# A transformer block on one core: the first product of the second gate/up pass by a second Strassen level, woven into the unit in front, and both F tiles evacuated jointly

## The chip, the cores and the metric

One core of a Trainium2 chip. The metric is device time in microseconds of the whole kernel. Repeats of one kernel scatter by about 1 us.

## The reference

Input 2048 tokens of width D = 1024. A linear-attention block is followed by a gated block, and this case is about the gated block:

```python
x = A_x
h = x + _A_ref(_layernorm(x), A_wqkv, A_wo)
h2 = h + _B_ref(_layernorm(h), B_W_gate, B_W_up, B_W_down)
# _B_ref:  gate = x @ W_gate;  up = x @ W_up      (1024 x 3584 each)
#          gate = gate * (gate > 0)
#          out  = (gate * up) @ W_down            (3584 x 1024)
```

## The kernel before

Strassen's scheme replaces eight block products by seven, at the price of block sums. The kernel uses it for almost all large products. The gate/up product runs in two passes over 1024 tokens each, and each pass has 14 **units**, alternately a gate unit and an up unit. A unit makes seven products P1 to P7 for a pair of F tiles (u = 0, 1), each of eight matmuls of 128x512 (four for each tile), which end in PSUM banks. Copies between banks ("fk1", "fk2") let two results share a partial sum.

In the second pass P5 is itself done by Strassen (the **inner** level: two weight tiles by two halves of K by two halves of the tokens): seven sub-products M1 to M7 of two 128x256 matmuls each, 14 narrow ones instead of eight wide ones. Cut to its order, the unit before is:

```python
sub(cX, B_X, B_(0, 0), A(0, 0), True, "M1")      # sub: 2 matmuls of 256 columns
sub(cD, B_D, G(0), XS(0), False, "M5")
ident_act(c0, cX, ...)                           # ScalarE, "M1c"
p1(0); p1(1)         # prod P1: 4 matmuls of 512 columns; then fk1: bank BA[u] copied to BB[u]
sub(cX, ..., "M6");  s5(1, 0, cX, ...)
sub(c0, ..., "M2")
p2(0)                # P2 on top of P1 in BA[0], evacuated by "h11"
sub(cX, ..., "M7");  s5(1, 1, cX, ...);  s5_add(1)
p6(0); p2(1); p6(1)  # P6 on top of the copy in BB[u]; then fk2: BB[u] copied to BC_[u]
sub(cX, ..., "M4");  sub(cD, ..., "M3")
... # M4c, s5_add(0)
for u in range(2):   # P7 into BB[u], evacuated by "c22" tile by tile (VectorE, + P5's result)
    prod(u, BB[u], t_blk(u, 2), s_blk(2), False, "P7")
    evac5(1, 1, u, bank(BB[u]), B_bank[BB[u]], c22, B_c22, "c22")
... # P3 into BC_[u], evacuated by "c12" in the same way
for u in range(2):   # P4 on top of P7 in BB[u], evacuated by "h21"
    prod(u, BB[u], t_blk(u, 3), a_blk(1, 1), False, "P4")
    evac(0, 1, u, BB[u], "h21")
```

Gate units evacuate with ScalarE's relu. Up units evacuate on VectorE, multiplying by the gate values. VectorE further makes the weight sums of the next unit in between. Every matmul is issued by one helper, so all have one source line (L769 before, L777 after).

Of the kernel before, what the change touches and what calls it, by code (L numbers as in the profile page):

```python
# [132 lines left out]
def bass_sequential_preLN__linear_attn_block__glu_gated_reglu__prompt_kernel(  # L133
# [71 lines left out]
    with es:  # L205
# [90 lines left out]

        RO = sb("RO", [P, NTR * 4 * KH * P], bf16)
# [9 lines left out]
        lx = RW[:, 4 * NW:8 * NW].bitcast(f16).rearrange("p (z j c) -> p z j c", z=2, j=4)  # L307
        sg_g = [RWG[:, x:x + 4 * WDW].bitcast(f16).rearrange("p (j m t) -> p j m t", j=4, t=SHB)
# [12 lines left out]
        RX = sb("RX", [P, (2 * NHR + NOS) * NW], bf16)  # L321
# [118 lines left out]
        B_s5q = [bufs("s5q%d_" % i, 2) for i in range(2)]  # L440
        B_xs5 = bufs("xs5_", 4)
        B_out2 = bufs("out2_", STB)
        B_xr = bufs("xr_", 2)
# [71 lines left out]
        for b_ in B_outst:  # L515
            b_.over = B_E + B_bt + [B_TWq[2]]
        for b_ in B_hnE:
            b_.over = B_o + B_oT
# [152 lines left out]
        def x_wsums(m):  # L671
# [12 lines left out]
            def one():  # L684
                dma(sl_rx[z], r_v[:, 1, :, m, :], xr[:, z].rearrange("p k (h c) -> p (k h) c", c=HNW), "st_rx_%d" % m,
                    reads=[B_xr[z]], writes=B_rscr[1][2 * m:2 * m + 2])
                add(0, q_(0, 1), q_(0, 0))
                add(2, q_(1, 1), q_(0, 1))
# [697 lines left out]
        def x_inner():  # L1386
            def A(t, k):
                return Ssum[:, 0, 2 * k:2 * k + 2, t * SHB:(t + 1) * SHB], [B_S[0]]

            def X(j):  # L1390
                return xs5[:, j], [B_xs5[j]]

            def add(j, x, y, op):
                PL.add("dve", lambda e: e.tensor_tensor(out=xs5[:, j], in0=x[0], in1=y[0], op=op), reads=x[1] + y[1],
                       writes=[B_xs5[j]], name="xs%d" % (j + 1))
            return [lambda: add(0, A(1, 0), A(1, 1), ALU.add), lambda: add(1, X(0), A(0, 0), ALU.subtract),
                    lambda: add(2, A(0, 0), A(1, 0), ALU.subtract), lambda: add(3, A(0, 1), X(1), ALU.subtract)]
# [22 lines left out]
        def ffn_unit(ps_, n, fill, mid):  # L1420
            Lg = (ps_ * NPAIR + n) * 2
# [5 lines left out]
            if ps_ in L2F:  # L1427
                BE, BB = BB, BE
            if up:
                BB, BC_ = BC_, BB  # L1430
            z = n % 2
            fl = (1, 1) if ps_ not in L2F or n == NPAIR - 1 else (1, 0) if up else (2, 1)

# [27 lines left out]
            def prod(u, b, st_, mov, start, name):  # L1461
                (sf, sr), (mf, mr) = st_, mov
                for kk in range(KH):
                    mm(bank(b), sf(kk), mf(kk), start and kk == 0, kk == KH - 1, sr + mr, B_bank[b],
                       "%s%s_%d_%d" % (name, "gu"[up], ps_, n), skip=True)
# [33 lines left out]

            if ps_ in L2F:  # L1500
                cX, cD, c0 = ps[:, BE[1], 0:SHB], ps[:, BE[1], SHB:2 * SHB], ps[:, BE[0], 0:SHB]
                B_X = B_D = B_bank[BE[1]]
                tb = [B_T[kt[0]][0], B_T[kt[1]][0]]

                def sub(dst, bdst, w, x, start, name):
                    for kk in range(2):
                        mm(dst, w[0](kk), x[0](kk), start and kk == 0, kk == 1, w[1] + x[1], bdst,
                           "%s_%d_%d" % (name, ps_, n), skip=True)

                def B_(kh, u):  # L1510
                    return (lambda kk: Tring[:, kt[u], 0, 2 * kh + kk, :]), [tb[u]]

                def G(j):
                    return (lambda kk: g5[:, z, j, kk * P:(kk + 1) * P]), [B_g5[z][j]]

                def A(t, k):
                    return (lambda kk: Ssum[:, 0, 2 * k + kk, t * SHB:(t + 1) * SHB]), [B_S[0]]

                def XS(j):
                    return (lambda kk: xs5[:, j, kk, :]), [B_xs5[j]]  # L1520

                def s5(u, t, src, b, name):
                    ident_act(ftmp[:, u, t * SHB:(t + 1) * SHB], src, [], [b, B_s5q[u][t]], name)

                def s5_add(t):
                    d = ftmp[:, 1, t * SHB:(t + 1) * SHB]
                    PL.add("dve", lambda e: e.tensor_tensor(out=d, in0=cD, in1=d, op=ALU.add), reads=[],
                           writes=[B_D, B_s5q[1][t]], name="s5a%d" % t)
                for u in range(2):
                    for t in range(2):  # L1530
                        B_s5q[u][t].over = [B_s5[u]]

                sub(cX, B_X, B_(0, 0), A(0, 0), True, "M1")
                sub(cD, B_D, G(0), XS(0), False, "M5")
                ident_act(c0, cX, [], [B_X, B_bank[BE[0]]], "M1c")
                p1(0)
                p1(1)
                sub(cX, B_X, G(1), XS(1), False, "M6")
                s5(1, 0, cX, B_X, "M6c")
                sub(c0, B_bank[BE[0]], B_(1, 0), A(0, 1), False, "M2")  # L1540
                fillin(2 if up else 3)
                p2(0)
                go(mid[2])
                sub(cX, B_X, G(2), XS(2), False, "M7")
                s5(1, 1, cX, B_X, "M7c")
                s5_add(1)
                p6(0)
                p2(1)
                p6(1)
                go(mid[0])  # L1550
                sub(cX, B_X, G(3), A(1, 1), False, "M4")
                sub(cD, B_D, B_(1, 1), XS(3), False, "M3")
                e_ = ps[:, BE[0]:BE[0] + 2, 0:SHB]
                PL.add("act", lambda e: e.activation(out=ftmp[:, 0, :].rearrange("p (t c) -> p t c", t=2), in_=e_,
                                                     func=ACTF.Identity), reads=[B_bank[BE[0]]],
                       writes=[B_X, B_s5[0]], name="M4c")
                go(later)
                later.clear()
                fillin(2 if up else 3)
                s5_add(0)  # L1560
                B_s5[1].over = B_s5q[1]
                B_s5[1].w = B_s5q[1][0].w
            else:
                p1(0)
                p1(1)
                fillin(1)
                for u in range(2):
                    prod(u, BE[u], t_blk(u, 0), s_blk(0), True, "P5")
                    ident_act(ftmp[:, u, :], bank(BE[u]), [B_bank[BE[u]]], [B_s5[u]], "s5")
                fillin(1)  # L1570
                p6(0)
                p6(1)
                go(later)
                later.clear()
                fillin(1)
                go(mid[0])
                p2(0)
                go(mid[2])
                p2(1)
                fillin(1)  # L1580
# [6 lines left out]
            fillin(fl[0])  # L1587
# [9 lines left out]
            fillin(fl[1])  # L1597
# [3 lines left out]
            if ps_ > 0 or n < NPAIR - 2:  # L1601
                load_w_next()
                load_w_next()

# [51 lines left out]
        def down_pass(ps_, fill):  # L1656
# [256 lines left out]
            else:  # L1913
                claim(B_W, B_hnT)
                at(0, 3, *l2_sums(q_10, sg_rg2, "sg2", NM - 1, NM))
# [228 lines left out]
        L2F = (1,)  # L2144
# [3 lines left out]
        for p_ in range(NPASS):  # L2148
            fill = []
            for q in range(NPAIR):  # L2150
                if q + 1 < NPAIR:
                    t_ = t_sums((p_ * NPAIR + q + 1) * 2)
                    if p_ in L2F:
                        t_ = t_[0:1] + w_inner(q + 1) + t_[1:]
                    fill = fill + t_
                mid = [[], [], [], [], []]
                if q > 0 and q % 2 == 0:
                    mid[0].append(lambda q=q: hh_sums(q - 2))
                    mid[3].append(lambda q=q: hh_sums(q - 1))
                if p_ == 0:  # L2160
# [15 lines left out]
                    else:  # L2176
# [5 lines left out]
                        else:  # L2182
                            mid[0] = [load_wd_next] * 2 + mid[0] + [w0_, w1_]
                else:
                    if q == 0:
# [3 lines left out]
                    if 1 <= q <= NM:  # L2189
                        w0_, w1_ = x_wsums(q - 1)  # L2190
                        mid[0].append(w0_)
                        mid[1].append(w1_)
                    if q == NPAIR - 1:
                        claim(B_sgg, B_w[2:6])
                        g_ = l2_sums(q_10, sg_rg2, "sg2", 0, NM - 1)
                        mid[0] += g_[0:2]
                        mid[1] += g_[2:4]
                ffn_unit(p_, q, fill, mid)
                if p_ == 1 and q == NM + 1:
                    claim(B_wd[0:NWS - 3], B_xr + flat(B_lx))  # L2200
                    wd_lim[0] = len(WLIST)
                    for _ in range(NWS):
                        load_wd_next()
                if p_ == 1 and q == NPAIR - 1:
                    for i in range(NWX):
# [6 lines left out]
            hh_sums(NPAIR - 2)  # L2212
            hh_sums(NPAIR - 1)
            if p_ in L2F:
                claim(B_V, B_xs5 + flat(B_g5))
            late = []
            if p_ + 1 < NPASS:
# [13 lines left out]
                if p_ + 1 in L2F:  # L2231
                    def claim_xs():
                        claim(B_xs5, B_V)
                        claim(flat(B_g5), B_V)

                    gi = w_inner(0)
                    xi = x_inner()
                    late += [(claim_xs, (6, 0)), (xi[0], (6, 3)), (xi[1], (6, 4)), (xi[2], (6, 4)), (xi[3], (6, 5))]
# [61 lines left out]
```

## Time and profile before

| | before |
|---|---|
| median of the first runs | 722.53 us (722.41 to 722.60) |
| span of the profiled run | 720.5 us |
| PE, VectorE (DVE), ScalarE (ACT) busy | 99%, 82%, 50% |
| second gate/up pass, by PE starts | 474.37 to 640.81 us: 166.44 us |
| one unit of it | 11.89 us |
| granted clock of PE | 1.0 |

How to read it: a PE that is 99% busy says little by itself, since matmul records overlap and their ends are modelled. What says that PE issues without a gap is that the distance between starts equals the number of columns at the full rate.

### The profile page before, as it was taken

How to read it: one execution, taken by the hardware profiler on the slowest of the kernel's cores; microseconds unless marked ns; L12 is line 12 of the kernel's file. 1: busy time of each engine (PE TensorE's matmuls, PEld its weight loads, DVE VectorE, ACT ScalarE, POOL GpSimd, SP SyncE). 2: the span in 40 equal slices, each digit the busy share in tenths (PEclk: the TensorE clock that was granted, in tenths of full speed). 3: DMA queues.
4: the chain of work that ended last, by engine and by line, in shares of the span. 5: the costliest groups of instructions: out<-in, count | busy, mean ns of one | idle time of the engine just before them, and what ended most of it. 6: DMA issues, size and time to landing. Idle time of an engine off the chain costs nothing.

```text
span 720.5 us, 12877 instructions
## 1 busy us (share of the span) xinstructions
PE 714.3 (99%) x4901; PEld 380.0 (53%) x4901; DVE 588.9 (82%) x1030; ACT 358.9 (50%) x626; POOL 110.8 (15%) x178
## 2 busy tenths in 40 slices
PE   8999999999999999999999999999999999999998
PEld 3344444444444444444444568865555555447887
DVE  6988867899776889888988787887889877888885
ACT  4977666764842466677756111035455445423010
POOL 3321100000350103332321001310000000000331
PEclk9999999999999999999999999999999999999999
DMA  9852344015998797999998999994554572037997
GB/s 295 260 113 65 38 136 157 9 30 97 216 202 264 222 284 236 276 320 297 296 281 266 313 251 317 318 215 119 145 169 139 160 245 84 1 95 248 322 323 183
DMA packets 195101, 144.17 MB, mean 200 GB/s; under 512 B 53984, under 2 KB 172512, under 8 KB 195040
## 3 DMA queue, kind: packets, MB, share of 16 engines
q1 hardware_dynamic: 190048, 138.77, 65.9%
q0 software_dynamic: 4032, 3.67, 3.6%
q10 hardware_dynamic: 960, 0.92, 0.4%
q8 instruction: 38, 0.62, 0.4%
q14 instruction: 23, 0.19, 0.1%
HBM read 98.76 MB, written 32.51 MB: 182 GB/s over the span
## 4 chain that ended last, share of the span: by engine, by line
PE 95%; DVE 2%; DMA 1%; ACT 1%; issue 1%; SPq 0%; ACTq 0%
PE ps L769 95%; DMA RAB<-in_A_wqkv_dram 1%; DVE RWG L1016 0%; DVE RE L857 0%; DVE RX L1100 0%; DVE RE L1674 0%; DVE RX L854 0%; DVE RH L1016 0%; ACT RXH L809 0%; DVE RC L991 0%; DVE RW L991 0%; ACT ps L774 0%; PE ps L910 0%; DVE RWG L1614 0%; SPq L567 0%
## 5 line engine op out<-in xcount | busy, mean ns | idle before, releaser
L774 ACT ACTIVATE ps<-ps 128x512 f32<-128x512 f32 (+1 forms) x193 | 108.9, 565 | 220.8 <-PE ps L769 212.1
L769 PE MATMUL ps<-RC,RO 128*128 128x512 f16 x616 | 143.0, 369 | 0.0
L769 PE MATMUL ps<-RH,RWG 128*128 128x512 bf16 x448 | 108.1, 379 | 0.0
L769 PEld LDWEIGHTS ps<-RC,RO 128*128 128x128 f16 x616 | 60.3, 98 | 63.5
L769 PE MATMUL ps<-RC,RWG 128*128 128x512 f16 x320 | 76.9, 379 | 0.3 <-ACT ps L774 0.2
L769 PEld LDWEIGHTS ps<-RH,RWG 128*128 128x128 bf16 x448 | 43.8, 98 | 46.9
L1483 DVE TENSOR_TENSOR RAB<-ps,RAB 128x512 bf16<-128x512 f32 x56 | 37.3, 686 | 31.3 <-PE ps L769 31.3
L769 PE MATMUL ps<-RH,RO 128*128 128x512 bf16 (+1 forms) x256 | 61.2, 379 | 0.0
L1683 POOL DMA_DIRECT2D out_dram<-RX x20 | 17.9, 1281 | 263.7 <-DVE RX L1674 221.5
L769 PE MATMUL ps<-RW,RE 128*128 128x512 bf16 x256 | 57.6, 380 | 0.0
L769 PE MATMUL ps<-RW,RAB 128*128 128x256 f16 (+3 forms) x362 | 52.9, 301 | 0.0
L769 PEld LDWEIGHTS ps<-RC,RWG 128*128 128x128 bf16 (+1 forms) x320 | 30.0, 98 | 40.3 <-ACT ps L774 6.3
L774 ACT ACTIVATE RE<-ps 128x512 f32<-128x512 f32 (+1 forms) x64 | 31.5, 503 | 37.8 <-PE ps L769 37.8
L769 PE MATMUL ps<-RAB 128*128 128x512 bf16 (+2 forms) x238 | 49.8, 348 | 0.0
L769 PEld LDWEIGHTS ps<-RW,RAB 128*128 128x128 f16 (+1 forms) x362 | 35.3, 98 | 14.5
L1674 DVE TENSOR_TENSOR RE<-ps,RE 128x512 f32<-128x512 f32 x44 | 30.2, 686 | 14.2 <-PE ps L769 13.7
L774 ACT ACTIVATE RAB<-ps 128x512 bf16<-128x512 f32 x56 | 33.3, 595 | 16.7 <-PE ps L769 16.4
L1367 DVE TENSOR_TENSOR RO<-RWG 128x1024 f16<-128x1024 bf16 x54 | 36.9, 684 | 4.5 <-DMA RWG<-in_B_W_up_dram 4.5
L769 PEld LDWEIGHTS ps<-RH,RO 128*128 128x128 f16 (+1 forms) x256 | 24.4, 98 | 29.9 <-ACT RX L774 1.5
L1478 ACT ACTIVATE RAB<-RAB 128x1024 bf16<-128x1024 bf16 x28 | 29.5, 1055 | 19.3 <-DVE RAB L1469 18.7
L1469 DVE TENSOR_TENSOR RAB<-ps,RE 128x512 bf16<-128x512 f32 x56 | 37.1, 685 | 2.1 <-PE ps L769 1.7
L769 PEld LDWEIGHTS ps<-RW,RE 128*128 128x128 bf16 x256 | 24.0, 98 | 27.9 <-DVE RXH L1265 0.4
(170 smaller groups left out, 1170.3 us busy)
## 6 DMA issues: line engine op xcount, KB each, us to landing
RWG<-in_B_W_gate_dram SPq DMA_DIRECT2D x28, 512.0 KB, 6.2
RWG<-in_B_W_up_dram SPq DMA_DIRECT2D x28, 512.0 KB, 5.2
RW<-l_scr SPq DMA_DIRECT2D x20, 448.0 KB, 5.6
RW<-in_B_W_down_dram SPq DMA_DIRECT2D x14, 512.0 KB, 5.4
t_scr<-RW SPq DMA_DIRECT2D x14, 512.0 KB, 4.8
l_scr<-RX SPq DMA_DIRECT2D x7, 1024.0 KB, 6.1
RE<-l_scr SPq DMA_DIRECT2D x15, 448.0 KB, 4.9
RE<-in_A_x_dram SPq DMA_DIRECT2D x23, 256.0 KB, 3.7
```

What stands on the lines that cost most here:

```text
L769: lambda e: e.matmul(out_ap, lhsT, rhs, start=start, stop=stop, skip_group_check=skip),
L774: PL.add("act", lambda e: e.activation(out=dst, in_=src, func=func), reads=reads, writes=writes, name=name)
L1367: PL.add(eng, lambda e: e.tensor_tensor(out=tb(j, u), in0=f0(u), in1=f1(u), op=ALU.subtract), reads=[B_w[i + x] for x in r] + ([B_T[k + x] ...
L1469: PL.add("dve", lambda e: e.tensor_tensor(out=d, in0=src, in1=ftmp[:, u, :], op=ALU.add), reads=[bsrc, B_s5[u]], writes=[db], name=name)
L1478: PL.add("act", lambda e: e.activation(out=d, in_=d, func=ACTF.Relu), reads=[], writes=db, name=name)
L1483: PL.add("dve", lambda e: e.tensor_tensor(out=d, in0=bank(b), in1=d, op=ALU.mult), reads=[B_bank[b]], writes=[db], name=name)
L1674: PL.add(eng, lambda e: e.tensor_tensor(out=dst, in0=in0, in1=in1, op=op), reads=reads, writes=writes, name=name)
L1683: PL.add("pool", lambda e: e.dma_start(dst, src, accum_op=ALU.add), reads=[bsrc], writes=[B_hscr[st]], slot=sl, name="acc_%d_%d" % (st, dh))
```

## The change

Its intent: P1 of units 1 to 13 also gets the inner Strassen level (seven sub-products R1 to R7), which takes 512 columns a unit off PE. R1 to R7 are spread over the unit in front, so that the copies between them are covered by other products. To make room on VectorE for the added sums, the two F tiles of a result are evacuated in one instruction, and the PSUM reads of the up units' h11 and h21 go to ScalarE, leaving VectorE a 16-bit multiply.

The core of the diff (buffers, the wide D1/D3 sums of `hh_pair` and the new places of load and sum calls are cut):

```diff
+        def w_inner1(n): ...      # three VectorE sums of the raw weights of unit n: g1
+            go(pre)
             sub(cX, B_X, B_(0, 0), A(0, 0), True, "M1")
-            sub(cD, B_D, G(0), XS(0), False, "M5")
+            sub(cD, B_X, G(0), XS(0), False, "M5")
...
-                p1(0)
-                p1(1)
+            go(late21)                       # h21 of the unit in front
+            if n == 0:                       # only unit 0 still makes its own P1
+                for u in range(2):
+                    prod(u, BA[u], w_blk(u, 0, 0), a_blk(0, 0), True, "P1")
+                    fk1(u, BB)
+            if n > 0:
+                p2()
... # M6, M2, M6c, out11(0), P6(0), fk2(0), M7, M3, s5a
+            if nxt:
+                sub(r0, B_r, Br(0, 0), Ar(0, 0), True, "R1")
+                sub(rX, B_r, Gr(0), XSr(0), False, "R5")
+                ident_act(m5r, rX, [B_r], [B_m5r], "R5c")
+                ident_act(rX, r0, [], [B_r], "R1c")
... # P6(1), fk2(1), M4, out11(1), P7(0)
+                sub(r0, B_r, Br(1, 0), Ar(0, 1), False, "R2")
+                sub(rX, B_r, Gr(1), XSr(1), False, "R6")
+                ident_act(rc, rX, [B_r], [B_y], "R6c")
... # P7(1), c22 of both tiles, P3(0)
+                sub(rX, B_r, Gr(2), XSr(2), False, "R7")
+                sub(rc, B_y, Br(1, 1), XSr(3), False, "R3")
+                dve(... both R banks + m5r ..., "Ra")
... # P3(1), c12 of both tiles, P4(0)
+                sub(rX, B_r, Gr(3), Ar(1, 1), False, "R4")
+                for u in range(2):
+                    fk1(u, BC_)
+            prod(1, BB[1], t_blk(1, 3), a_blk(1, 1), False, "P4")
```

```diff
-                PL.add("dve", lambda e: e.tensor_tensor(out=d, in0=src, in1=ftmp[:, u, :], op=ALU.add), ...
+                dve(d, ps[:, bk[0]:bk[0] + 2, :], ftmp[:, 0:2, :], ...)      # c22, c12: both tiles
```

## The prediction

> **What bounds the kernel now.** I read the page first, then the chain of work that ended last, then the PE timeline of the second gate/up pass, then busy time by stretch. The page (busy time, then the chain by engine) and the chain in order of time:
>
> ```profile
> PE 714.3 (99%) x4901; PEld 380.0 (53%) x4901; DVE 588.9 (82%) x1030; ACT 358.9 (50%) x626; POOL 110.8 (15%) x178
> ...
> PE 95%; DVE 2%; DMA 1%; ACT 1%; issue 1%; SPq 0%; ACTq 0%
> ```
>
> ```profile
> 103.69 0.59 ACT ps L774
> 104.28 0.05 issue
> 104.32 576.26 PE ps L769 x3727
> 680.58 0.02 issue
> 680.60 0.69 DVE RE L1674
> ```
>
> PE works 714.3 of 720.5 us, and one unbroken piece of 576 us of matmuls covers everything this change touches. The second gate/up pass runs from 474.4 to 640.8 us: 14 units of one Strassen step. One whole unit on the PE timeline (start, length, engine, operation, count; the ends are modelled and overlap the next start, so I read starts):
>
> ```profile
> 486.26 0.38 PE L769 MATMUL ps<-RC,RO 128*128 128x256 f16 x2
> 486.48 0.38 PE L769 MATMUL ps<-RE 128*128 128x256 f16 x2
> 486.69 1.89 PE L769 MATMUL ps<-RH,RWG 128*128 128x512 bf16 x8
> 488.42 0.38 PE L769 MATMUL ps<-RE 128*128 128x256 f16 x2
> 488.64 0.38 PE L769 MATMUL ps<-RC,RO 128*128 128x256 f16 x2
> 488.86 1.03 PE L769 MATMUL ps<-RH,RWG 128*128 128x512 bf16 x4
> ...
> 494.69 1.89 PE L769 MATMUL ps<-RC,RWG 128*128 128x512 f16 x8
> 496.42 1.89 PE L769 MATMUL ps<-RH,RO 128*128 128x512 bf16 x8
> 498.15 0.38 PE L769 MATMUL ps<-RC,RO 128*128 128x256 f16 x2
> ```
>
> The line of eight wide matmuls at 486.69 is P1, the product to be changed. Eight 128x512 matmuls take 488.42-486.69 = 1.73 us, 0.2157 each; a pair of 128x256 takes 0.218 us, 0.109 each. A unit is 48 wide and 14 narrow ones: 48 x 0.2157 + 14 x 0.109 = 11.88 us, and the trace has 498.15-486.26 = 11.89. So PE issues with no gap at all, and only fewer columns can shorten this pass. The other engines, unit by unit and then over ten units (stretch, its length, busy us and count of each engine, clock, DMA share, GB/s):
>
> ```profile
> 486.26:498.15 11.89, 11.89 (x64) 6.08 (x63) 7.18 (x15) 5.32 (x10) 0.00 (x0) 1.00 0.30 90
> 498.15:510.04 11.89, 11.89 (x64) 6.07 (x63) 10.90 (x25) 6.61 (x12) 0.00 (x0) 1.00 0.54 154
> 521.93:640.81 118.88, 118.88 (x622) 60.64 (x621) 97.55 (x197) 59.68 (x110) 0.00 (x0) 1.00 0.42 124
> ```
>
> VectorE is the second engine, 97.55/118.88 = 82% busy; ScalarE has half its time free.
>
> **What the Trainium skill says.** "TensorE: Matmul & The Clock Gate", section "Wait — 56ns, not 53.3ns?": start to start is N/2.4 GHz plus about 2.5 ns. That gives 215.8 ns for 512 columns and 109.2 for 256; the trace's 0.2157 and 0.109 agree, and the narrow form pays its fixed 2.5 ns twice. "VectorE: DVE Perf Modes", section "The perf-mode tier table": tensor_tensor on 16-bit SBUF data runs two elements a cycle, with a PSUM operand one. The trace agrees: 1024 elements SBUF to SBUF 684 ns, 512 from PSUM 685 ns, 1024 from PSUM 1219 ns; so two 512 evacuations joined save 2 x 685 - 1219 = 0.15 us. "PSUM — Partial Sum Buffer", section "PSUM bank collisions raise a hardware error": PSUM is to be guarded by bank. The kernel does so (one tracker a bank), hence the new copies in one bank become waits of PE if they come late; nothing in the profile before shows the new ones.
>
> **The change part by part.**
> PE. In units 0 to 12 the P1 of the following unit (8 wide matmuls) becomes seven sub-products R1 to R7 of two narrow ones each; unit 0's own P1 stays direct. The built programs, counted by shape, agree: wide 2571 to 2467 (-104 = 13 x 8), narrow 1274 to 1456 (+182 = 13 x 14). Sum: -104 x 0.2157 + 182 x 0.1092 = -22.43 + 19.87 = **-2.56 us**. The nominal saving of an eighth of the columns is 8 x 0.2157/8 x 13 = 2.80; the fixed part of the extra instructions takes 0.24 back. All of it is on the path, as PE is the path.
>
> VectorE, with whole durations. Each unit gains three sums of the raw weights (0.42 + 2 x 0.29 = 1.0 us, 512, 256 and 256 elements) and Ra (0.69, 512 from PSUM). It loses 0.85 - 0.69 = 0.16 where two s5a of 256 become one of 512, and 0.30 where c22 and c12 are joined. An up unit further loses four evacuations of 685 with a multiply and gets two bf16 multiplies of 692 instead: 2.74 - 1.38 = 1.36 us saved, the PSUM read going to ScalarE. Joint D1/D3 sums save some 0.3 us per two units (4 x 0.42 against 2 x 0.69). Ledger after: gate unit 4 x 0.684 + 2 x 1.0 + 2 x 0.69 + 2 x 1.22 + 0.42 + 0.69 = 9.7 us; up unit 2.74 + 2.0 + 1.38 + 2.44 + 1.38 + 0.57 + 3 x 0.69 = 12.6; pair 22.3 of 2 x 11.69 = 23.4 us. Durations overlap in the trace by some 0.08 us an instruction, so busy time will be nearer 20 us, 85%. The up unit alone is over its length and spills into the next. It fits, without much room.
>
> ScalarE. Each unit has six 256-wide copies (0.38 us each) instead of three; an up unit gets P2's two 512-wide evacuations (0.60 each) and one joint 1024-wide one (estimate from the trace's 0.60: 0.60 + 512/1.2 GHz = 1.03). With four fork copies of 0.58, the 0.59 of M4c and a gate unit's two relus of 1.06, a pair sums to 17 us, 8.5 a unit of 11.69, against 5.3 to 6.6 before. Not a bound.
>
> Latencies. With the starts above and T = 0 at M1 of a unit, PE's slots are P2 from 0.44, M6 2.16, P6(0) 2.60, M7 3.46, R1 3.90, P6(1) 4.34, M4 5.20, P7(1) 6.72, Ra's inputs done 8.88, P3(1) to 9.75, R4 10.61, end 11.69. From the end of a matmul's issue to its reader's start the trace shows 0.26 us on ScalarE (488.42 to 488.68) and 0.20 on VectorE (489.72 to 489.92). Three loops decide:
> - M6 ends 2.38, copy M6c 2.64 to 3.02, needed by M7 at 3.46: 0.4 us spare.
> - M3 ends 3.90, s5a on VectorE 4.10 to 4.79, needed by M4 at 5.20: 0.4 spare, if VectorE is free at 4.1. After an up unit its queue holds h22, h12, two T sums, three weight sums and h21 from about -0.5 on: 5 x 0.6 + 1.0, less 0.5, is 3.5, and with the wait of h21 for its copy some 3.7 to 4.0. Close.
> - P3(1) ends 9.75, c12 9.95 to 11.17, fork copy fk1 11.2 to 11.8, needed by P2 at 12.13 (0.44 into the next unit): 0.3 spare.
> All three fit, so I expect few stalls; I allow 0.15 us in all.
>
> Transfers. Same bytes. But four of the seven early W_down loads now start after the last x sums of unit 13 instead of in unit 8. The stores they wait for land in 2.4 us, loads in about 5, so from some 3.5 us into unit 13 they land near its end; the fourth chunk is wanted 3 x 2.6 = 7.8 us after it. Hidden. The last down pass takes over three 1536-wide sums (some 3 us of VectorE), but its VectorE also starts earlier, since unit 13 has fewer of them.
>
> Sum: 722.53 - 2.56 + 0.15 = **720.1 us**, -0.3%.
>
> **The rivals.**
> 1. VectorE in order becomes the bound in up units: s5a or c12 comes a few tenths late and PE stalls at M4 or P2. For it: 12.6 us of ledger in an 11.69 us unit, spare of 0.3 to 0.4. Against: the pair has room, durations overlap. At 0.2 us a unit it takes the whole gain: 722.6; at 0.1, 721.4.
> 2. Late W_down loads stall the start of the last down pass. For: 3 slots full instead of 7; DMA share 0.95 later in that pass. Against: the arithmetic above, and nine slots of lead. A miss would cost 1 to 3 us: 721 to 723.
> 3. The joint evacuation frees VectorE and shortens other waits as well, giving more than 2.56. Against: PE has no gap in this pass to give back; in the last down pass only 0.18 us. So 719.8 at best.
>
> **Range and chances.** No outcome I can build moves the time by 2% (14.5 us): the column saving is 0.35%, and the stalls of rivals 1 and 2 together give 724. So 98% within 2%. The low end, 719.5, is the full gain plus what little gaps there are; the high end, 721.7, is rival 1 at 0.1 us a unit.
>
> **What will show it.** Right: unit period 11.69 us on the PE timeline; no PE idle between 474 and 638; last pass starting at about 638.3; VectorE around 85% there. Wrong: gaps of PE released by VectorE (s5a, c12) or ScalarE (M6c, fk1), above all in up units, or a gap released by a DMA near 646.

## The result, and the profile after

The changed kernel takes **719.82 us** (median of 4 runs, 719.75 to 720.06) against 722.57 for the kernel before in the same rounds. The ratio is 0.9963, with a 95% interval of 0.9946 to 0.998. Run again later with the experiments it took 719.58 against 722.67 (ratio 0.996).

The busy times and the chain by engine on the page of the changed kernel, then the chain in order of time:

```profile
PE 711.7 (99%) x4979; PEld 387.4 (54%) x4979; DVE 597.4 (83%) x1009; ACT 383.9 (53%) x679; POOL 110.4 (15%) x178
...
PE 93%; DVE 3%; DMA 2%; issue 1%; SPq 0%; ACT 0%; ACTq 0%
```

```profile
104.65 0.05 issue
104.70 573.81 PE ps L777 x3807
678.50 0.02 issue
```

The one long piece of matmuls is still unbroken, and it is 576.26 - 573.81 = 2.45 us shorter, although it holds 80 more matmul records (3807 against 3727). PE remains the path. One gate unit of the changed kernel on the PE timeline (start, length, engine, operation, count):

```profile
499.98 0.38 PE L777 MATMUL ps<-RC,RO 128*128 128x256 f16 x2
500.20 0.38 PE L777 MATMUL ps<-RE 128*128 128x256 f16 x2
500.42 1.89 PE L777 MATMUL ps<-RH,RWG 128*128 128x512 bf16 x8
502.14 0.38 PE L777 MATMUL ps<-RE 128*128 128x256 f16 x2
...
503.88 0.38 PE L777 MATMUL ps<-RH,RWG 128*128 128x256 bf16 x2
504.10 0.38 PE L777 MATMUL ps<-RX 128*128 128x256 f16 x2
504.32 1.03 PE L777 MATMUL ps<-RC,RO 128*128 128x512 f16 x4
...
510.59 0.38 PE L777 MATMUL ps<-RH,RX 128*128 128x256 bf16 x2
510.81 1.03 PE L777 MATMUL ps<-RH,RO 128*128 128x512 bf16 x4
511.67 0.38 PE L777 MATMUL ps<-RC,RO 128*128 128x256 f16 x2
```

The eight wide matmuls at 500.42 are now P2; P1 is gone from this place. R1 (weights RWG) and R5 (sums in RX) stand at 503.88 and 504.10, R4 at 510.59, each 0.218 us long by starts. The unit takes 511.67 - 499.98 = 11.69 us, which is 40 x 0.2157 + 28 x 0.1092 = 11.69: no gap. Busy time by stretch, one up unit and then ten units:

```profile
511.67:523.36 11.69, 11.69 (x69) 6.64 (x68) 10.48 (x20) 7.62 (x16) 0.00 (x0) 1.00 0.49 138
511.67:628.57 116.90, 116.90 (x681) 66.53 (x680) 104.45 (x187) 78.12 (x151) 0.00 (x0) 1.00 0.42 119
```

VectorE is now 104.45/116.90 = 89% busy (82% before), ScalarE 67%. VectorE does more work, and PE still doesn't wait for it.

**A sharper measure.** The pass lies between the first M1 and the first matmul of the last down pass. In the changed kernel these start at:

```profile
474.76 0.38 PE L777 MATMUL ps<-RC,RO 128*128 128x256 f16 x2
...
638.73 5.34 PE L777 MATMUL ps<-RE,RAB 128*128 128x512 bf16 x24
```

This gives a pass of 163.97 us against 166.44. The second profile of the same kernel gives 475.41 to 639.38, again 163.97. So the pass repeats to 0.01 us, while the time at which it begins moves from 474.1 to 475.7 us between the profiles of all kernels, and the stretch behind it takes 79.5 to 79.7 us in each. So the scatter of the totals arises before this pass, and where two runs differ by a few tenths the pass length decides. It fell by 2.47 us, while the medians fell by 2.75. About 0.1 us more lies behind the pass: the stretch there takes 79.69 us before, and 79.51 to 79.60 in the changed kernel and in every edit of it below.

### The profile page after: what moved, and what is told of

The parts are those of the page before. It is cut to its first block, busy times and chain, and to the rows that moved or that the text cites. A ratio compares the mean times of both kernels' runs of the same rounds, so it can differ in the third digit from the quotient of the medians.

```text
span 718.3 us, 13075 instructions
## 1 busy us (share of the span) xinstructions
PE 711.7 (99%) x4979; PEld 387.4 (54%) x4979; DVE 597.4 (83%) x1009; ACT 383.9 (53%) x679; POOL 110.4 (15%) x178
## 4 chain that ended last, share of the span: by engine, by line
PE 93%; DVE 3%; DMA 2%; issue 1%; SPq 0%; ACT 0%; ACTq 0%
PE ps L777 93%; DMA RE<-in_A_x_dram 1%; DMA RAB<-in_A_wqkv_dram 1%; DVE RW L999 1%; DVE RC L999 1%; SPq L573 0%; DVE RWG L1024 0%; DVE RE L865 0%; DVE RX L1108 0%; DVE RE L1850 0%; DVE RX L862 0%; DVE st L791 0%; DVE RH L1024 0%; DVE RWG L1790 0%; ACT RX L858 0%
## 5 line engine op out<-in xcount | busy, mean ns | idle before, releaser
L782 ACT ACTIVATE ps<-ps 128x512 f32<-128x512 f32 (+1 forms) x233 | 122.3, 531 | 200.5 <-PE ps L777 171.8
L777 PE MATMUL ps<-RH,RWG 128*128 128x512 bf16 (+1 forms) x396 | 91.2, 365 | 0.0
L777 PE MATMUL ps<-RC,RWG 128*128 128x512 f16 x320 | 79.0, 379 | 0.5 <-ACT ps L782 0.4
L782 ACT ACTIVATE RE<-ps 128x512 f32<-128x512 f32 (+3 forms) x85 | 49.3, 597 | 39.1 <-PE ps L777 28.9
L777 PE MATMUL ps<-RH,RO 128*128 128x512 bf16 (+1 forms) x256 | 63.3, 379 | 0.0
L777 PEld LDWEIGHTS ps<-RH,RWG 128*128 128x128 bf16 x396 | 38.7, 98 | 40.9 <-ACT ps L782 0.2
L1850 DVE TENSOR_TENSOR RE<-ps,RE 128x512 f32<-128x512 f32 x44 | 30.2, 687 | 15.1 <-PE ps L777 12.4
L1623 DVE TENSOR_TENSOR RE<-ps,RE 128x512 f32<-128x512 f32 (+1 forms) x28 | 26.8, 958 | 14.1 <-PE ps L777 14.1
L1375 DVE TENSOR_TENSOR RO<-RWG,RO 128x1024 f16<-128x1024 bf16 x54 | 37.0, 685 | 0.5
L782 ACT ACTIVATE RAB<-ps 128x512 bf16<-128x512 f32 (+1 forms) x49 | 32.1, 654 | 5.6 <-PE ps L777 5.3
L862 DVE TENSOR_SCALAR RX<-RX 128x512 bf16<-128x512 bf16 x64 | 18.4, 288 | 19.5 <-ACT RX L858 18.6
```

Of the source, the lines that this page charges most:

```text
L777: lambda e: e.matmul(out_ap, lhsT, rhs, start=start, stop=stop, skip_group_check=skip),
L782: PL.add("act", lambda e: e.activation(out=dst, in_=src, func=func), reads=reads, writes=writes, name=name)
L862: PL.add("dve", lambda e: e.tensor_scalar(out=Et[:, k, :], in0=Et[:, k, :], scalar1=1.0, scalar2=1e-6, op0=ALU.min, op1=ALU.add), reads=[] ...
L1375: PL.add(eng, lambda e: e.tensor_tensor(out=tb(j, u), in0=f0(u), in1=f1(u), op=ALU.subtract), reads=[B_w[i + x] for x in r] + ([B_T[k + x] ...
L1623: PL.add("dve", lambda e: e.tensor_tensor(out=dst, in0=in0, in1=in1, op=op), reads=reads, writes=writes, name=name)
L1850: PL.add(eng, lambda e: e.tensor_tensor(out=dst, in0=in0, in1=in1, op=op), reads=reads, writes=writes, name=name)
```

## The experiments

Twelve runs, the changed kernel again and eleven edits of it. All gave correct results. **Theory**: the gain is only the columns that PE no longer streams. The weave and the joint evacuation gain nothing by themselves; they keep the added copies and sums out of PE's way. **Rivals**: the evacuation or the freer VectorE gives part of the gain; VectorE's total load, not the place of its work, decides.

| run | median us | ratio to before | pass, us |
|---|---|---|---|
| before | 722.27, 722.43, 722.67 | 1 | 166.44 |
| changed kernel, again | 719.58 | 0.996 | 163.97 |
| P1 direct in its own unit | 730.36 | 1.011 | 174.30 |
| P1 direct in its own unit, tile by tile | 727.71 | 1.0069 | 171.65 |
| P1 direct, woven | 722.50 | 1.0 | 166.54 |
| R in one block | 772.13 | 1.0686 | 217.61 |
| evacuation all split | 720.10 | 0.9969 | 164.44 |
| c22, c12 split | 719.60 | 0.9962 | 163.97 |
| all products narrow | 721.54 | 0.9989 | 165.37 |
| pad in front of s5a, 0.6 us | 719.81 | 0.9966 | 163.97 |
| pad in front of c12, 0.6 us | 720.85 | 0.9978 | 164.77 |
| pad in front of c12, 1.13 us | 727.78 | 1.007 | 171.71 |
| W_down loads late | 720.31 | 0.9975 | 163.97 |

### P1 direct in its own unit

```diff
-            if n == 0:
-                for u in range(2): prod(u, BA[u], ..., "P1"); fk1(u, BB)
+            for u in range(2): prod(u, BA[u], ..., "P1"); fk1(u, BB)
-            if nxt: ... R1 to R7, their copies and sums
```

> R1 to R7 and their weight and token sums taken out, every P1 direct again (8 wide matmuls); joint evacuation, sums and load order of the change kept. Theory (the gain is the columns of PE alone): unit back to 11.89 us, PE without gaps, 722.4 us (722.0 to 722.9). Rival (the joint evacuation or freer VectorE gives part of it): well under the kernel before, 721.5 or less.

Measured: 730.36 us, 8 us above the kernel before. Both views missed. The PE timeline (first two lines) and the VectorE timeline (third) of an up unit show why:

```profile
520.06 1.89 PE L777 MATMUL ps<-RC,RWG 128*128 128x512 f16 x8
522.38 1.67 PE L777 MATMUL ps<-RH,RO 128*128 128x512 bf16 x7 [0.43 <-DVE RE L1623]
```

```profile
520.88 2.40 DVE L1623 TENSOR_TENSOR RE<-ps,RE 128x1024 bf16<-128x1024 f32 x2
```

Without R2, R6, R7 and R3 between them, P7, P3 and P4 follow each other at once, and P4 waits for the joint c22, which is the first of the two in the VectorE line. One record of P4 is missing (seven of eight), so the 522.38 is its second matmul. Without a gap that one would start 1.73 + 0.22 after 520.06, at 522.01; the gap is 0.37 us, not the 0.43 printed. Further gaps stand in front of P2 (0.22, behind fk1) and M4 (0.16 in this unit). The narrow sub-products also serve as **filler** that covers evacuation, so this run changed two things at once. Two more runs separate them.

### P1 direct in its own unit, evacuated tile by tile

```diff
+            evac5(1, 1, BB, c22, B_c22, "c22", 0)
             prod(1, BB[1], t_blk(1, 2), s_blk(2), False, "P7")
-            evac5(1, 1, BB, c22, B_c22, "c22")
+            evac5(1, 1, BB, c22, B_c22, "c22", 1)      # c12 in the same way
```

> As the run with P1 direct in its own unit (730.4 us), but c22 and c12 evacuated tile by tile, tile 0 right behind its own product. If the P4 gap of that run (0.33 us in a gate unit, 0.4 in an up unit) comes from the joint c22 ending too late for P4 of tile 0, this gap goes and the waits of P2 (0.22) and M4 (0.1 to 0.15) stay: 14 x 0.35 = 5 us less, 725.5 us (724.5 to 727). If it comes from VectorE's queue alone: no change, 730.

Measured: 727.71 us, 2.65 better than the run above (the passes, 171.65 and 174.30, differ by as much), half of what was expected and outside the expected range. The gap at P4 is gone: the up unit starts that second P4 matmul at 522.33, which is 1.95 after its P3, as it should be. The size was off because I had read the gap from a line with a missing record; it was 0.37 us in an up unit and 0.12 in a gate unit. The P2 and M4 gaps stayed. So joint evacuation has a price, a later c22, and in the changed kernel the filler pays it.

### P1 direct, woven at the places of R

```diff
-                sub(r0, ..., "R1"); sub(rX, ..., "R5"); ... "R5c"; "R1c"
+                n1(0, 0)        # two wide matmuls of the next unit's P1, tile 0
... # n1(0, 2) at R2/R6, n1(1, 0) at R7/R3, n1(1, 2) at R4; no copies, no sums, no Ra
```

> The next unit's P1 stays direct (8 wide matmuls) but is woven into the unit in front at the places of R1 to R7; joint evacuation and all else of the change kept, the sums and copies of R gone. This isolates the arithmetic of PE, which the run with P1 direct in its own unit did not (there the P4, P2 and M4 waits came back). Theory: unit 11.89 us, no gaps, 722.4 us, 2.56 above the change in the same rounds (2.2 to 3.0). Rival (the weave or the joint evacuation gives part of the gain): under 721.5. Rival (a direct P1 stalls in any order here): over 724.

Measured: 722.50 us, 2.92 above the changed kernel in the same rounds, and level with the kernel before (ratio 1.0). The pass on its PE timeline:

```profile
641.46 4.91 PE L777 MATMUL ps<-RE,RAB 128*128 128x512 bf16 x22
```

With M1 at 474.92 in this profile the pass is 166.54 us, 2.57 longer than the 163.97 of the change; the prediction's arithmetic was 2.56. Same weave, same joint evacuation, only the arithmetic of P1 differs. This **shows** that the gain in the pass is PE's columns and nothing else, and that weave and joint evacuation alone are worth nothing there. (Both woven kernels have the small stall of unit 0 that is described below, hence 166.54 and not 166.44. The 0.1 us behind the pass is kept without R, so it isn't P1's; what brings it was not tested.)

### R in one block behind the unit

```diff
-            ... R1 to R7 between P6 and P4
             prod(1, BB[1], t_blk(1, 3), a_blk(1, 1), False, "P4")
+            if nxt: R1, R5, R5c, R1c, R2, R6, R6c, R7, R3, Ra, R4, fk1
```

> The seven sub-products not woven into the unit but in one block behind its last product, same work. Theory (each copy R1c, R6c, Ra, fk1 becomes a wait of PE, some 0.26 to 0.2 us start lag plus 0.38, 0.38, 0.69 and 0.58 us of work): about 2.8 us a unit on 13 units, 756 us (745 to 765), the second pass bound by waits for ScalarE and VectorE. Rival (PE's queue or the narrow matmuls hide most of them): under 730.

Measured: 772.13 us. The waits of PE in one block (what ended them stands in brackets):

```profile
536.38 0.39 PE L777 MATMUL ps<-RH,RWG 128*128 128x256 bf16 x2 [0.88 <-ACT ps L782]
...
537.45 0.39 PE L777 MATMUL ps<-RX 128*128 128x256 f16 x2 [0.46 <-ACT ps L782]
...
539.28 0.39 PE L777 MATMUL ps<-RH,RX 128*128 128x256 bf16 x2 [1.22 <-DVE ps L1623]
...
540.41 1.90 PE L777 MATMUL ps<-RH,RWG 128*128 128x512 bf16 x8 [0.30 <-ACT ps L782]
```

They are the four that were named: R1c, R6c, Ra, fk1. From start to start PE loses 1.03, 0.62, 1.38 and 0.46 us here, 3.5 in all, against about 2.8 expected; a gate unit loses 3.1. Over 13 units that is some 43 of the 53.6 us by which the pass is longer. The rest is the M4 and P4 waits of the first experiment, which come back when the filler leaves the unit (some 5 us), and a lower granted clock: 0.98 over 523 to 630 us, and 0.91 over 480 to 520, where a unit takes 16.4 to 16.5 us and not the 15.1 to 15.4 of the quick ones. I estimate some 6 us for the clock, as what is left of the 53.6. No other run shows a lower clock in this pass, and why it fell stays open. Ra in the block shown began later behind R3 than the 0.20 us allowed; that stays open too. The order of identical work is worth 52 us here, twenty times the gain, clock included.

### Evacuation split

All of it (c22 and c12 tile by tile, h11 and h21 of up units on VectorE straight from PSUM), and c22 and c12 alone:

```diff
-                dve(d, ps[:, bk[0]:bk[0] + 2, :], ftmp[:, 0:2, :], ...)
+                for u in range(2):
+                    dve(d[:, u], bank(bk[u]), ftmp[:, u, :], ...)
-                    ident_act(c12[:, u, :], bank(BA[u]), ..., "h11c")      # only in the first run
+                    dve(d[:, u], bank(BA[u]), d[:, u], ..., "h11", ALU.mult)
```

> R kept, joint evacuation undone: c22 and c12 tile by tile, h11 and h21 of up units by VectorE straight from PSUM, as before the change. Theory (joint evacuation brings no gain of its own but keeps VectorE out of PE's way): VectorE busy near 97% in the second pass; R1 of an up unit waits some 0.35 us for h11 on VectorE, 7 times: 722.3 us (721.3 to 723.5), most of the gain lost. Rival (VectorE has room either way): 719.8.

> Only c22 and c12 evacuated tile by tile (two of 685 ns in place of one of 1219), h11 and h21 as in the change. Theory: 0.30 us more VectorE work a unit, within its idle time; c12 of tile 0 is even done sooner, so no PE gap: 719.8 us (719.5 to 720.3). Rival (joining these is what lets the change fit): over 721.

Measured: 720.10 and 719.60 us. Splitting c22 and c12 costs nothing (pass 163.97). Splitting h11 and h21 as well costs 0.5 us (pass 164.44): R1 of an up unit starts at 515.86 where 515.78 was due, and five of the up units take 11.78 us and not 11.69; the first one shows no loss. The expected 0.35 us in each of 7 units was too much: VectorE's h11, which R1 waits for, ends at 515.80. VectorE is 110.27/118 = 93% busy there, not 97%. Joining c22 and c12 didn't even free VectorE: over 512 to 630 us it is busy for 105.25 us when they are split and 105.52 when they are joined. So joint evacuation is an insurance of half a microsecond, and all of it lies in h11 and h21; it is not what lets the change fit.

### All wide products as narrow ones

```diff
-                    mm(bank(b), sf(kk), mf(kk), ...)
+                    for h_ in range(2):                    # two halves of 256 columns
+                        mm(bank(b)[:, c_], sf(kk), mf(kk)[:, c_], ...)
```

> Every wide product of the second pass as twice as many 256-column matmuls, same columns: 568 wide ones become 1136 narrow. Theory (a narrow one costs 0.1092 us, half a wide one plus about 1.3 ns): 568 x 0.0027 = +1.5 us, 721.3 us (720.9 to 721.8), no gaps. Rival (weight loads of 98 ns no longer hide under narrow ones): over 723. Other rival (no fixed cost): 719.8.

Measured: 721.54 us, pass 165.37: 1.40 us for 568 more instructions, 2.5 ns each, with no gap. This measures the term that took 0.24 us off the nominal gain. Weight loads still hide.

### Pads on VectorE

One 16-bit add more in each unit, in front of s5a or in front of c12:

```diff
+            PL.add("dve", ... tensor_tensor(out=out2[:, 0:2, :], in0=hnT[...], in1=hnT[...], op=ALU.add) ..., name="pad")
             evac5(1, 0, BC_, c12, B_c12, "c12")
```

> One 1024-element 16-bit add (0.60 us of VectorE) more in each of the 14 units, in front of s5a. In the trace VectorE idles 0.54 to 0.65 us there and s5a ends 0.34 us before M4 wants it. Theory (in-order spare by place decides): no gap, 719.8 us (719.5 to 720.3), VectorE 94% busy. Rival (VectorE's total load decides): 0.3 us a unit or more, over 722.

> The same add in front of c12 instead. VectorE idles 0.16 to 0.23 us there, and fk1 of tile 0 ends some 0.3 us before P2 wants it, so 0.46 to 0.53 spare against 0.60: theory 0.1 us of gap at P2 in each of 13 units, 721.1 us (720.3 to 722.3), gap released by ScalarE (fk1). Rival (VectorE's total load decides): same as the pad in front of s5a.

> A 2048-element 16-bit add (1.13 us) in front of c12 in each unit, where the 0.60 us one cost 0.06 us of PE a unit. So the spare there is 0.54 us and the rest goes straight to PE: 1.13 - 0.54 = 0.59 us in each of 13 units, +7.7: 727.5 us (726 to 730), the gap at P2. Rival (the pad displaces idle time elsewhere in VectorE and PE catches up): under 723.

Measured: 719.81, 720.85 and 727.78 us. The same 0.6 us of work costs nothing in front of s5a (pass 163.97, VectorE 111.21 of 118 us = 94% busy), and 0.80 us of the pass in front of c12, where VectorE is no busier (109.78 us). Busy time by stretch, pad in front of s5a and then the same pad in front of c12:

```profile
512.00:630.00 118.00, 118.00 (x688) 67.09 (x686) 111.21 (x198) 79.15 (x154) 0.00 (x0) 1.00 0.41 118
```

```profile
512.00:630.00 118.00, 118.00 (x684) 65.92 (x683) 109.78 (x197) 77.78 (x152) 0.00 (x0) 1.00 0.41 117
```

P2 in the run with the small pad in front of c12, and then with the large one:

```profile
511.64 0.38 PE L777 MATMUL ps<-RE 128*128 128x256 f16 x2
511.91 1.90 PE L777 MATMUL ps<-RH,RWG 128*128 128x512 bf16 x8
```

```profile
513.10 0.38 PE L777 MATMUL ps<-RE 128*128 128x256 f16 x2
513.90 1.90 PE L777 MATMUL ps<-RH,RWG 128*128 128x512 bf16 x8 [0.42 <-ACT ps L782]
```

P2 should follow M5 by 0.22 us; it follows by 0.27 and by 0.80. The unit grows from 11.69 to 11.75 and to 12.29 us. So the spare in front of c12 is about 0.54 us, and everything beyond goes to PE one for one. The release by ScalarE is fk1, which waits for c12. VectorE's place, not its load, decides.

### W_down loads late

```diff
-                if p_ == 1 and q == NPAIR - 3:      # three loads in unit 11, four in unit 13
+                if p_ == 1 and q == NPAIR - 1:      # all seven in unit 13
```

> All seven early W_down loads only after the last x sums of unit 13, instead of three in unit 11. Theory (loads hidden with room): first lands 4 to 5 us after about 633, wanted at 638.7; 719.8 us (719.5 to 721.0), at most a gap of 0.5 us at the start of the last down pass. Rival (load timing is near the edge): 721 to 724 with a gap released by DMA.

Measured: 720.31 us, pass 163.97, and the last down pass starts without a gap at 638.91. Its profile shows the first of these loads issued at 631.7 us rather than at 633, because only the last four wait for the x sums. The 0.5 us above the other runs lies outside the stretch that the edit touches, within the scatter of the kernel. The transfers are hidden.

## Why the prediction was right

- **PE, -2.56 us**: right. The woven direct P1 gives 2.57 for the arithmetic alone. Against the kernel before the pass fell by 2.47; the 0.1 that is missing is the stall of the next point. The starts to read it from were in the trace before.
- **Stall allowance, 0.15 us**: right in size, but by luck as to the place. It was meant for the three loops, which stall nowhere. Unit 0 takes 474.76 to 488.29 = 13.53 us where 48 x 0.2157 + 28 x 0.1092 = 13.41 are due, in front of M6 (0.06) and P2 (0.03): ScalarE starts the first copy of the pass only at 476.26, behind a VectorE sum of the down pass in front. The other units have no gap.
- **VectorE ledger**: the order of size was right, but the "85%" was too low: 89%. It took too much overlap off the durations: the 37 instructions of a pair make 22.3 us in the ledger and 20.9 in the trace, 0.04 us each and not 0.08. The 0.30 us a unit for joining c22 and c12 were not there either (see the split runs). ScalarE's 17 us a pair measured 7.93 + 7.62 = 15.6. The up unit did not spill over as forecast either: the windows show 10.4 us in a gate unit and 10.5 in an up unit, since the multiplies that end an up unit are done in the next one.
- **The three spares**: right as a bound. For c12 I counted only the 0.3 us behind it. In the changed kernel c12 starts at 509.93 after VectorE idled 0.16, and fk1 begins at once behind it:

```profile
509.93 1.23 DVE L1623 TENSOR_TENSOR RAB<-ps,RE 128x1024 bf16<-128x1024 f32 x1 [0.16 <-PE ps L777]
```

```profile
511.18 1.07 ACT L782 ACTIVATE ps<-ps 128x512 f32<-128x512 f32 x2 [1.04 <-DVE RAB L1623]
```

  The first of the two copies (0.58 us) ends at 511.76; P2 starts at 511.67 + 0.44 = 512.11, so 0.35 is left behind it. With the idle time in front, 0.16 to 0.23, that makes the 0.5 that the pads measured. For s5a the idle time in front is 0.54 to 0.65, with 0.34 to 0.41 behind; the pad of 0.6 us fits into that and doesn't measure it. M6c ends 0.5 us before M7 starts (502.93 and 503.44), and no run padded it.
- **Rival 1** (VectorE late) fell: it needs more than 0.5 us extra in front of c12. **Rival 2** (late loads) fell, although the late loads were issued at 633.49, 4.9 us into unit 13 and not 3.5. **Rival 3** (more than 2.56) fell: in the woven run the joint evacuation gained nothing. The medians differ by 2.75 to 3.1 us. Of the excess over 2.47 about 0.1 lies behind the pass; the rest is no larger than the scatter of repeats, and no profile shows it: in the first profile of the changed kernel the pass even begins 0.39 us later than before.
- The prediction missed in one thing that was not asked of it: it did not see that R1 to R7 are also the filler that covers the joint evacuation.

No run clearly beat the changed kernel. The one with c22 and c12 split (719.60) equals it, with the same pass length.

## What to carry to other kernels

Where PE issues without a gap at the full clock, count columns and a fixed 2.5 ns for each matmul: the gain of cutting work was known here to 0.1 us before the run, and the question is only whether each added copy and sum ends before PE wants its bank. Answer that by place, not by busy share: add up the idle time in front of the instruction and the spare behind it; a pad of known length measures the sum. And when a step is taken out to isolate another, check whether it was also filler: replace it by equal work at the same places.

## What the Trainium skill lacked or had wrong

- "Perfetto Trace Analysis", section "Per-instruction lifecycle: what the profiler-reported window actually captures", names the propagation of a semaphore but, for a matmul's reader, gives no time. Here a reader starts 0.26 us (ScalarE) and 0.20 us (VectorE) after the last matmul's issue ends, read in the trace before, and these two numbers enter every loop of the prediction.
- "TensorE: Matmul & The Clock Gate", section "Wait — 56ns, not 53.3ns?": its fixed 2.5 ns holds. The section has it from 128 and 512 columns; the run with all products narrow adds 256 columns, with 568 instructions more (1.40 us).
- "VectorE: DVE Perf Modes", section "The DRAIN you can't avoid", has the next instruction start only when the pipe is empty, and finds that a semaphore after each of eight copies costs nothing. It gives no figure for a neighbour that has to wait for the result in front of it: in the changed kernel a 1024-element sum is followed after 0.60 us by an independent one (504.69 to 505.29) and after 0.72 us by one that reads its result (505.29 to 506.01).
- "Perfetto Trace Analysis", section "Matmuls", advises rotating banks so that evacuation overlaps the next group. It says nothing of using another unit's products as filler between groups that share a bank; the block run, which loses that filler and puts the copies of R in PE's way, is 52 us slower than the changed kernel, some 6 of them with a lower clock.
